# Attention pieces of batches 0 and 1 in another order, in a fused sparse-attention and feed-forward kernel

## The chip, the cores and the metric

The kernel runs on one core of a Trainium2 chip. The core has TensorE for matrix products (PE in the profile, PEld for its weight loads), VectorE (DVE), ScalarE (ACT), GpSimd (POOL) and a queue for transfers (SP), each with its own instruction stream. The metric is the time of one execution on the device in microseconds (us). The kernel before takes 332.97 us (median of three runs, 332.66 to 333.33). A profile of one execution covers a span of 331.5 us; all positions below are counted from the start of that span.

## The reference

Eight batches of eight heads, 576 positions, head dimension 64. Heads 0 to 3 attend to the last 32 positions (local), heads 4 to 7 to earlier positions with the same index modulo 32 (strided). The result goes through a feed-forward layer with a PReLU-like activation.

```python
    scores = scale * np.matmul(q, k.transpose(0, 1, 3, 2))
    pos = np.arange(S)
    rel = pos[:, None] - pos[None, :]
    mask_local = (rel >= 0) & (rel < stride)          # heads 0..3
    mask_strided = (rel >= 0) & (pos[None, :] % stride == pos[:, None] % stride)
    ...
    attn = attn / (np.sum(attn, axis=-1, keepdims=True) + 1e-09)
    return np.matmul(attn, v).astype(np.float32)
...
    h = x @ w_in            # x: (4608, 512), w_in: (512, 2048)
    g = np.maximum(h, 0.0) + alpha * np.minimum(h, 0.0)
    return (g @ w_out).astype(np.float32)
```

## The kernel before, in words

**Units and pairs.** A batch has two units, strided and local, of four heads each. A unit has two pairs of heads; pair g belongs to batch g // 4, and `P.hp` = g % 4 says which (0 and 1 local, 2 and 3 strided). The output of a pair fills one of the four 128-row slabs of `xT`, the input of the feed-forward layer, for the 576 columns of its batch.

**Pieces.** The attention work is cut into closures, the pieces:

- `T(u, "q")`, `T(u, "k")` (`transpose_piece`, L235): eight TensorE transposes of a unit's q or k into a PSUM tile `tp`, then copies to SBUF (`qT`, `kT`). In batches 0 and 1 (`NEARLY = 2`) the copy is in two halves, one for each pair, one on DVE and one on ACT. With k come the last 64 positions (`tails`, PSUM tile `tt`, L258 and L263).
- `Sc(g, i)` (`score_piece`, L295): half of a pair's scores; in batches 0 and 1 the mask is added by two more matmuls (L311). ACT computes the exponential into one of six `et` tiles (L316, L319).
- `Pv(g, i)` (`pv_piece`, L345): probabilities times V, with a column of ones that gives the sum; then DVE's reciprocal `rc` (L352) and division into `x16` (L354). A strided pair has three such pieces, a local pair two.
- `X(g)` (`x_piece`, L362): transposes of `x16` into a PSUM tile `xp`, and a copy to `xT`: on ACT for strided pairs (L366), on DVE for local ones (L370).
- `over_v` (L189): a DVE copy of 32 rows inside the local V tile, which the local PVs read.

The PSUM tiles `tp`, `tt`, `pv` and `xp` share one pool of three buffers (tag `ps`), so each new one needs an old one to be read to its end.

**Order.** `keep` holds every engine's instructions in the order in which the program writes them. The order of pieces for batches 0 and 1 is written out by `alone(u0, u1, ahead)`, called with the strided unit as u0, the local one as u1 and `ahead` true: transposes and scores of the strided unit, transposes of the local unit, scores of its first pair, all six strided PVs, scores of the second local pair, both strided X, the four local PVs (`over_v` ahead of the first), both local X.

**Around it.** Batch 0's pieces run alone on TensorE; after each, `warm` puts matmuls that only keep TensorE busy (`wps`, L608; one of 512 columns from the third piece on). Before the fifth piece DVE casts batch 0's strided V (`cast_v`). Then comes the feed-forward layer in nine chunks of 512 tokens. Its first product is `lin1_piece` (16 pieces of four matmuls into `hps`, L544; ACT's negative part L554, DVE's combination L557). The second is `lin2_piece` (16 pieces of four matmuls into `ops`, L586, with ACT's `osb` copy at each fourth, L591). Batch 1's pieces run between the `lin2` pieces of chunk 0: none after the first, two after each of the next nine, one after each of the last six, and what is left at the end. Later batches are interleaved with later chunks by another loop, which the change doesn't touch.

Of the kernel before, what the change touches and what calls it, by code (L numbers as in the profile page):

```python
# [31 lines left out]
def kernel(  # L32
# [10 lines left out]
    nc = tc.nc  # L43
    keep = tc.keep_in_program_order

    B, H, S, D = q.shape
# [36 lines left out]
    xT = cpool.tile([128, 4, RING], F16)  # L83
# [89 lines left out]
    def cast_copy(eng, o, i):  # L173
        if eng == "act":
            keep(nc.scalar.copy(o, i))  # L175
        elif eng == "dve":
            keep(nc.vector.tensor_copy(o, i))  # L177
        else:
            keep(nc.gpsimd.tensor_copy(o, i))  # L179
# [9 lines left out]
    def over_v(b, eng):  # L189

        v16 = vls[b % 2]
        cast_copy(eng, v16[0:32, 1:24, :], v16[96:128, 0:23, :])
# [7 lines left out]
    NEARLY = 2  # L200

    def make_pair(g):
        P = Pair()
        P.g, P.b, P.hp = g, g // 4, g % 4
        P.strided = P.hp >= 2
        P.pr = P.hp % 2
        P.n, P.w = (8, 72) if P.strided else (6, 96)
        u = g // 2
        P.dx = P.b >= DX and P.strided
        P.xd = P.b >= DX and P.hp < 3  # L210
        if P.dx:
            P.qT, P.kT = (z[u % 2].rearrange("r e c -> r (e c)") for z in (qTs, kTs))
        else:
            P.qT, P.kT = qTs[u % 2][:, g % 2], kTs[u % 2][:, g % 2]
        P.sgroups = ([0, 1, 2, 3], [4, 5, 6, 7]) if P.strided else ([0, 1, 2], [3, 4, 5])
        P.pgroups = ([0, 1, 2], [3, 4, 5], [6, 7]) if P.strided else P.sgroups
        P.et = {}
        P.x16 = None
        return P

    def transpose_piece(u, nm):

        b, strided = u // 2, u % 2 == 1
        early = b < NEARLY
        src = cast16[(b, strided, nm)]
        dst = qTs[u % 2][:, :, 0:576] if nm == "q" else kTs[u % 2][:, :, 32:608]  # L230
        tp = pspool.tile([128, 8, 64, 2], F16, tag="ps", name="tp")
        for j in range(8):
            blk = (src[:, j % 2, 128 * (j // 2) : 128 * (j // 2) + 128] if strided
                   else src[:, j].rearrange("p f d -> p (f d)"))
            keep(nc.tensor.transpose(tp[:, j].rearrange("r p e -> r (p e)"), blk, ident))  # L235
        if strided:
            main = tp.rearrange("r j p e -> r e j p")
            o = dst.rearrange("r e (j p) -> r e j p", j=8)[:, :, :, 0:64]
        else:
            main = tp.rearrange("r t p e -> r e p t")  # L240
            o = dst[:, :, 0:512].rearrange("r e (p t) -> r e p t", t=8)
        if early:
            for e in range(2):
                eng = "dve" if (nm == "q") == (e == 0) else "act"
                if nm == "k" and e == 1:
                    tails(b, u, strided)
                cast_copy(eng, o[:, e : e + 1], main[:, e : e + 1])
            return
        cast_copy("dve" if nm == "q" else "act", o, main)
        if nm == "k":  # L250
            tails(b, u, strided)
# [79 lines left out]
    def pv_piece(P, a):  # L331
        if P.x16 is None:
            if P.xd and P.strided:
                P.x16 = x16s
            else:
                P.x16 = xpool.tile([128, 1024], F16, tag="x16", name="x16")
        v16 = cast16[(P.b, P.strided, "v")]
        grp = P.pgroups[a]
        r = 72 if P.strided else 128
        pv = pspool.tile([128, 512], F32, tag="ps", name="pv")  # L340
        nb = 2 * len(grp)
        for x in range(nb):
            t, hh = grp[x // 2], x % 2
            et, c = P.et[(t, hh)]
            keep(nc.tensor.matmul(  # L345
                pv[:, 65 * x : 65 * x + 65], et[0:r, c : c + 128],
                v16[0:r, 2 * P.pr + hh, t, :] if P.strided else v16[:, 6 * (2 * P.pr + hh) + t, :],
                start=(x == 0), stop=(x == nb - 1), skip_group_check=True))
        w = P.w
        rc = rpool.tile([128, 8], F32, tag="rc", name="rc")  # L350
        pvv = pv[0:w, 0 : 65 * nb].rearrange("r (c e) -> r c e", e=65)
        keep(nc.vector.reciprocal(rc[0:w, 0:nb], pvv[:, :, 64]))  # L352
        c0 = 128 * grp[0]
        keep(nc.vector.tensor_tensor(  # L354
            P.x16[0:w, c0 : c0 + 64 * nb].rearrange("r (c e) -> r c e", e=64),
            pvv[:, :, 0:64],
            rc[0:w, 0:nb].unsqueeze(2).to_broadcast([w, nb, 64]), op=ALU.mult))

    def x_piece(P):
        xp = pspool.tile([128, 1024], F16, tag="ps", name="xp")  # L360
        for t in range(P.n):
            keep(nc.tensor.transpose(  # L362
                xp[:, P.w * t : P.w * t + P.w], P.x16[0 : P.w, 128 * t : 128 * t + 128], ident[0 : P.w, 0 : P.w]))
        base = (P.b % 4) * S
        if P.strided:
            keep(nc.scalar.copy(  # L366
                xT[:, P.hp, base : base + S].rearrange("r (p t) -> r p t", t=8),
                xp[:, 0:576].rearrange("r (t p) -> r p t", t=8)))
        else:
            keep(nc.vector.tensor_copy(xT[:, P.hp, base : base + S], xp[:, 0:576]))  # L370

    def x_dma(P):
        base = (P.b % 4) * S
# [14 lines left out]
    pairs = [make_pair(g) for g in range(npair)]  # L388
    pieces = []

    def feed(fn, g):
        pieces.append((g, fn))

    def T(u, nm):
        return lambda: transpose_piece(u, nm)

    def Sc(g, i):
        return lambda: score_piece(pairs[g], i)

    def Pv(g, i):  # L400
        return lambda: pv_piece(pairs[g], i)

    def X(g):
        return lambda: x_piece(pairs[g])

    def alone(u0, u1, ahead):

        A, L = (2 * u0, 2 * u0 + 1), (2 * u1, 2 * u1 + 1)
        feed(T(u0, "q"), -1)
        feed(T(u0, "k"), -1)  # L410
        for g in A:
            for i in range(2):
                feed(Sc(g, i), -1)
        if ahead:
            feed(T(u1, "q"), -1)
            feed(T(u1, "k"), -1)
            for i in range(2):
                feed(Sc(L[0], i), -1)
        for g in A:
            for i in range(3):  # L420
                feed(Pv(g, i), -1)
        if not ahead:
            feed(T(u1, "q"), -1)
            feed(X(A[0]), -1)
            feed(T(u1, "k"), -1)
            feed(X(A[1]), -1)
            for i in range(2):
                feed(Sc(L[0], i), -1)
        for i in range(2):
            feed(Sc(L[1], i), -1)  # L430
        if ahead:
            for g in A:
                feed(X(g), -1)
        for g in L:
            for i in range(2):
                if g == L[0] and i == 0:
                    feed(lambda: (over_v(u0 // 2, "dve"), pv_piece(pairs[L[0]], 0)), -1)
                else:
                    feed(Pv(g, i), -1)
        for g in L:  # L440
            feed(X(g), -1)

    alone(1, 0, True)
    end0 = len(pieces)
    alone(3, 2, True)
    end1 = len(pieces)


# [307 lines left out]
```

The softmax here doesn't subtract the row's maximum and nothing guards it: scores larger than these inputs give would overflow.

## Time and profile before

| engine | busy us | share of the span |
|---|---|---|
| PE | 319.1 | 96% |
| PEld | 161.6 | 49% |
| DVE | 183.0 | 55% |
| ACT | 171.8 | 52% |
| POOL | 141.2 | 43% |

Batch 0's pieces up to the last strided score take PE to 13.8 us. Its remaining pieces run from there to 27.2 us, where the first full `lin1` chunk sets in. That chunk takes PE to 40.9 us; batch 1's pieces lie between 42.5 and 66.6 us. A matmul's record shows its start well, while its end is modelled; a chain piece such as "PE tp L235 x8" gives the time by which eight matmuls move the chain on. "ACT kT L175 waited for" means that the engine named first stood until that instruction ended. Line 175 is the ACT branch and line 177 the DVE branch of the copy helper, so these lines are told apart by the tile's name.

### The profile page before, as it was taken

What the parts mean: (1) busy time and instruction counts of PE and PEld (TensorE: products, weight loads), DVE (VectorE), ACT (ScalarE), POOL (GpSimd) and SP (SyncE); (2) the same over time, 40 slices, a digit from 0 to 9 for tenths busy, and PEclk for the clock granted to TensorE, in tenths of its full rate; (3) what the DMA queues carried; (4) which work ended last, traced back from release to release, by engine and by line L of the source; (5) the groups of instructions that cost most, each with busy time, mean ns of one, the idle gap of its engine ahead of it and who ended that gap; (6) DMA issues with size and microseconds to landing.
All of it is one profiled execution on the core that took longest, in us unless ns stands there. A gap on an engine that the chain in (4) does not pass through costs nothing.

```text
span 331.5 us, 6272 instructions
## 1 busy us (share of the span) xinstructions
PE 319.1 (96%) x2493; PEld 161.6 (49%) x2493; DVE 183.0 (55%) x358; ACT 171.8 (52%) x297; POOL 141.2 (43%) x152
## 2 busy tenths in 40 slices
PE   7899999999998999999999999999999999999995
PEld 2554455554553445444458654445444444444444
DVE  5477836477544873387428832783368238605800
ACT  2644753458456645575457544764477237415611
POOL 7932495117986366736583628332611400000000
PEclk9999999999999999999999999999999999999999
DMA  7999999699599459774978397517730130011011
GB/s 221 194 205 206 248 207 154 109 211 210 105 159 179 163 69 162 122 203 55 172 114 216 37 153 125 106 17 106 139 57 18 51 96 21 1 74 52 2 63 63
DMA packets 77596, 40.32 MB, mean 122 GB/s; under 512 B 58480, under 2 KB 69248, under 8 KB 77568
## 3 DMA queue, kind: packets, MB, share of 16 engines
q0 software_dynamic: 41728, 17.38, 49.6%
q1 hardware_dynamic: 35840, 22.55, 29.9%
q8 instruction: 19, 0.31, 0.4%
q14 instruction: 9, 0.07, 0.1%
HBM read 38.01 MB, written 9.44 MB: 143 GB/s over the span
## 4 chain that ended last, share of the span: by engine, by line
PE 89%; ACT 4%; DVE 3%; DMA 2%; issue 1%; SPq 0%; ACTq 0%
PE hps L544 37%; PE ops L586 37%; PE sp L295 4%; PE pv L345 4%; PE tp L235 2%; DMA kl<-in_k_dram 2%; DVE x L354 1%; PE wps L608 1%; PE ops L577 1%; ACT xT L366 1%; ACT osb L591 1%; PE sph L311 1%; PE sp L311 1%; ACT kT L175 1%; DVE qT L177 1%
## 5 line engine op out<-in xcount | busy, mean ns | idle before, releaser
L544 PE MATMUL hps<-xT,win 128*128 128x512 f16 (+1 forms) x640 | 134.1, 358 | 3.4 <-ACT xT L366 2.8
L586 PE MATMUL ops<-wout,gT 128*128 128x512 f16 x560 | 137.0, 379 | 0.0
L557 DVE SCALAR_TENSOR_TENSOR gT<-neg,oma,hps 128x512 f16<-128x512 f32 x144 | 105.9, 744 | 51.3 <-ACT neg L554 43.6
L554 ACT ACTIVATE neg<-hps 128x512 f32<-128x512 f32 x144 | 86.0, 597 | 46.3 <-PE hps L544 45.2
L329 POOL TENSOR_TENSOR et<-et,consts 128x576 f16<-128x576 f16 (+1 forms) x48 | 61.1, 1275 | 94.3 <-ACT et L319 94.2
L544 PEld LDWEIGHTS <-win 128*128 128x128 f16 x640 | 59.6, 98 | 60.8 <-issue 7.3
L586 PEld LDWEIGHTS <-gT 128*128 128x128 f16 x560 | 48.3, 98 | 45.9
L319 ACT ACTIVATE et<-sp 72x576 f16<-72x576 f32 (+1 forms) x56 | 36.2, 646 | 30.9 <-PE sp L295 17.0
L591 ACT COPY osb<-ops 128x512 f32<-128x512 f32 x35 | 20.5, 586 | 49.9 <-PE ops L586 46.0
L352 DVE RECIPROCAL rc<-pv 72x6 f32<-72x6 f32 (+2 forms) x80 | 14.9, 186 | 55.0 <-PE pv L345 54.9
L354 DVE TENSOR_TENSOR x<-pv,rc 96x384 f16<-96x384 f32 (+2 forms) x62 | 33.0, 532 | 2.1
L345 PEld LDWEIGHTS <-et 72*128 72x128 f16 (+1 forms) x448 | 23.6, 98 | 16.8 <-DVE x L354 1.1
L295 PEld LDWEIGHTS <-kT 64*128 64x128 f16 x448 | 10.8, 95 | 26.2 <-issue 21.2
L295 PE MATMUL sp<-qT,kT 64*128 64x72 f16 (+1 forms) x392 | 17.0, 201 | 1.9 <-ACT kT L175 1.9
L608 PE MATMUL wps<-wrm 128*128 128x512 f16 x44 | 16.2, 442 | 1.2 <-DVE wrm L620 1.2
L177 DVE COPY qT<-tp 128x1024 f16<-128x1024 f16 (+1 forms) x10 | 10.1, 1010 | 11.7 <-PE tp L235 11.7
L167 POOL DMA_DIRECT2D vl<-in_v_dram x8 | 11.2, 1396 | 11.8 <-PE xp L362 10.5
L345 PE MATMUL pv<-vs,et 72*128 72x65 f16 x256 | 15.2, 194 | 0.1
L179 POOL COPY vs<-stv 72x1024 f16<-72x1024 f16 x14 | 14.4, 1034 | 0.0
L175 ACT COPY kT<-tp 128x1024 f16<-128x1024 f16 (+1 forms) x10 | 8.4, 843 | 7.4 <-PE tp L235 7.4
L383 ACT COPY xT<-xs 128x576 f16<-128x576 f16 x6 | 7.8, 1302 | 7.6 <-DMA xs<-x16s 7.6
L345 PE MATMUL pv<-vl,et 128*128 128x65 f16 x192 | 11.1, 194 | 0.0
(73 smaller groups left out, 162.9 us busy)
## 6 DMA issues: line engine op xcount, KB each, us to landing
out_dram<-osb SPq DMA_DIRECT2D x35, 256.0 KB, 2.3
ql<-in_q_dram SPq DMA_DIRECT2D x6, 512.0 KB, 5.9
kl<-in_k_dram SPq DMA_DIRECT2D x6, 512.0 KB, 6.3
stv<-in_v_dram POOLq DMA_DIRECT2D x8, 288.0 KB, 7.1
vl<-in_v_dram POOLq DMA_DIRECT2D x6, 384.0 KB, 10.6
win<-in_moe_w_in_dram POOLq DMA_DIRECT2D x4, 512.0 KB, 9.5
wout<-in_moe_w_out_dram POOLq DMA_DIRECT2D x4, 512.0 KB, 17.1
qsd<-in_q_dram POOLq DMA_DIRECT2D x6, 288.0 KB, 6.2
```

What stands on the lines that cost most here:

```text
L295: keep(nc.tensor.matmul(sps[y][:, w * x : w * x + w], P.kT[hf, k0 : k0 + 128], P.qT[hf, q0 : q0 + w], start=(x == 0), stop=(x == len(grp) ...
L319: keep(nc.scalar.activation(ev.rearrange("r (y c) -> r y c", y=2), sp[0:r, :, 0:n], AF.Exp, scale=SCALE))
L329: keep(nc.gpsimd.tensor_tensor(ev, ev, m, op=ALU.mult))
L345: keep(nc.tensor.matmul(pv[:, 65 * x : 65 * x + 65], et[0:r, c : c + 128], v16[0:r, 2 * P.pr + hh, t, :] if P.strided else v16[:, 6 * (2 * ...
L352: keep(nc.vector.reciprocal(rc[0:w, 0:nb], pvv[:, :, 64]))
L354: keep(nc.vector.tensor_tensor(P.x16[0:w, c0 : c0 + 64 * nb].rearrange("r (c e) -> r c e", e=64), pvv[:, :, 0:64], rc[0:w, 0:nb].unsqueeze ...
L544: keep(nc.tensor.matmul(hps[:, dst : dst + w], win16[:, kk, 128 * m : 128 * m + 128], xT[:, kk, src : src + w], start=(kk == 0 and x == 0) ...
L554: keep(nc.scalar.activation(neg, hps, AF.Relu, scale=-1.0))
L557: keep(nc.vector.scalar_tensor_tensor(gTs[n][:, m, :], neg, oma[:, m : m + 1], hps, op0=ALU.mult, op1=ALU.add))
L586: keep(nc.tensor.matmul(ops, gTs[n][:, kf, 128 * mt : 128 * mt + 128], wout16[:, kf, :], start=(kf == 0), stop=(kf == 15)))
L591: keep(nc.scalar.copy(osb, ops))
L608: keep(nc.tensor.matmul(wps, wrm[:, 0:128], wrm, start=True, stop=True))
```

## The change

`alone` loses its third parameter and writes one list. The strided PVs no longer come in one block: those of the first strided pair lie around the local transposes, those of the second between the local scores. `over_v` comes ahead of the second strided pair's first PV instead of the first local PV. Local PVs start ahead of the strided X pieces and alternate with them. In addition the `xT` copy of local pair 0 goes to ACT instead of DVE in batches 0 and 1. Which pieces exist, and how many, is as before.

Order of batch 0 and 1 from the seventh piece on (A0, A1: strided pairs; L0, L1: local pairs):

- before: Tq, Tk, Sc L0 (2), Pv A0 (3), Pv A1 (3), Sc L1 (2), X A0, X A1, over_v + Pv L0 (2), Pv L1 (2), X L0, X L1
- after: Pv A0, Tq, Pv A0, Tk, Pv A0, Sc L0 (2), over_v + Pv A1, Sc L1, Pv A1, Sc L1, Pv A1, Pv L0, X A0, Pv L0, X A1, Pv L1 (2), X L0, X L1

```diff
@@ x_piece
-            keep(nc.vector.tensor_copy(xT[:, P.hp, base : base + S], xp[:, 0:576]))
+            cast_copy("act" if P.b < NEARLY and P.hp == 0 else "dve",
+                      xT[:, P.hp, base : base + S], xp[:, 0:576])
@@ alone
-    def alone(u0, u1, ahead):
+    def alone(u0, u1):
 
         A, L = (2 * u0, 2 * u0 + 1), (2 * u1, 2 * u1 + 1)
-        feed(T(u0, "q"), -1)
-        feed(T(u0, "k"), -1)
-        for g in A:
-            for i in range(2):
-                feed(Sc(g, i), -1)
-        if ahead:
-            feed(T(u1, "q"), -1)
-            feed(T(u1, "k"), -1)
-            for i in range(2):
-                feed(Sc(L[0], i), -1)
-        for g in A:
-            for i in range(3):
-                feed(Pv(g, i), -1)
...
-        for i in range(2):
-            feed(Sc(L[1], i), -1)
-        if ahead:
-            for g in A:
-                feed(X(g), -1)
-        for g in L:
-            for i in range(2):
-                if g == L[0] and i == 0:
-                    feed(lambda: (over_v(u0 // 2, "dve"), pv_piece(pairs[L[0]], 0)), -1)
-                else:
-                    feed(Pv(g, i), -1)
-        for g in L:
-            feed(X(g), -1)
-
-    alone(1, 0, True)
+        fns = [T(u0, "q"), T(u0, "k")] + [Sc(g, i) for g in A for i in range(2)]
+        fns += [Pv(A[0], 0), T(u1, "q"), Pv(A[0], 1), T(u1, "k"), Pv(A[0], 2), Sc(L[0], 0), Sc(L[0], 1)]
+        fns += [lambda: (over_v(u0 // 2, "dve"), pv_piece(pairs[A[1]], 0)), Sc(L[1], 0), Pv(A[1], 1)]
+        fns += [Sc(L[1], 1), Pv(A[1], 2), Pv(L[0], 0), X(A[0]), Pv(L[0], 1), X(A[1])]
+        fns += [Pv(L[1], 0), Pv(L[1], 1), X(L[0]), X(L[1])]
+        for fn in fns:
+            feed(fn, -1)
+
+    alone(1, 0)
     end0 = len(pieces)
-    alone(3, 2, True)
+    alone(3, 2)
```

More of the change, by code (lines that the diff above doesn't have):

```diff
@@ L404, in X @@
         return lambda: x_piece(pairs[g])
-    def alone(u0, u1, ahead):
+    def alone(u0, u1):
         A, L = (2 * u0, 2 * u0 + 1), (2 * u1, 2 * u1 + 1)
-        feed(T(u0, "q"), -1)
-        feed(T(u0, "k"), -1)
-        for g in A:
-            for i in range(2):
-                feed(Sc(g, i), -1)
-        if ahead:
-            feed(T(u1, "q"), -1)
-            feed(T(u1, "k"), -1)
-            for i in range(2):
-                feed(Sc(L[0], i), -1)
-        for g in A:
-            for i in range(3):
-                feed(Pv(g, i), -1)
[L422 to L426, printed above, removed]
-            for i in range(2):
-                feed(Sc(L[0], i), -1)
-        for i in range(2):
-            feed(Sc(L[1], i), -1)
-        if ahead:
-            for g in A:
-                feed(X(g), -1)
-        for g in L:
-            for i in range(2):
-                if g == L[0] and i == 0:
-                    feed(lambda: (over_v(u0 // 2, "dve"), pv_piece(pairs[L[0]], 0)), -1)
-                else:
-                    feed(Pv(g, i), -1)
-        for g in L:
-            feed(X(g), -1)
-    alone(1, 0, True)
+        fns = [T(u0, "q"), T(u0, "k")] + [Sc(g, i) for g in A for i in range(2)]
[6 more added lines that the diff above has]
+    alone(1, 0)
     end0 = len(pieces)
-    alone(3, 2, True)
+    alone(3, 2)
     end1 = len(pieces)
```

## The prediction, written before the result was known

> **What bounds the kernel now.** I read the table of engines first, then the chain that ended last with its pieces in order of time, then the timeline and the waits of the stretch that the change rewrites.
>
> ```profile
> PE 319.1 (96%) x2493; PEld 161.6 (49%) x2493; DVE 183.0 (55%) x358; ACT 171.8 (52%) x297; POOL 141.2 (43%) x152
> ...
> PE 89%; ACT 4%; DVE 3%; DMA 2%; issue 1%; SPq 0%; ACTq 0%
> ```
>
> TensorE (PE) carries 89% of the chain. Only idle time of PE can be won, and after batch 0 there is little of it. So I look where the chain leaves PE, between 13.8 and 27.2 us, batch 0's own stage (start, length, piece):
>
> ```profile
> 13.81 0.46 PE tp L235 x8
> 14.29 0.70 DVE qT L177
> 15.02 0.59 ACT qT L175
> 15.61 0.50 ACT kT L175
> ...
> 18.26 0.55 DVE x L354
> 18.95 0.56 DVE x L354
> ...
> 25.70 0.56 DVE x L354
> 26.31 0.32 PE xp L362 x3
> 26.65 0.47 DVE xT L370
> 27.16 13.76 PE hps L544 x63
> ```
>
> There are three detours. The local scores follow the local transposes at once and wait for four copies. The divisions of six strided PVs come in one lump, and DVE serves one per 0.69 us (18.26 to 18.95). The last division, transposes and copy are a tail. The waits of 13.8 to 27.2 us agree (total, times, longest):
>
> ```profile
> PEld L362 <- DVE x L354: 1.3, 3, 0.5
> ...
> PEld L345 <- DVE x L354: 1.1, 4, 0.4
> PE sp L295 <- ACT kT L175: 0.9, 1, 0.9
> ```
>
> PE's work in this stretch, from the chain: 19 warm matmuls at 0.22 (4.1), two transpose pieces and a tail (0.92 + 0.12), four score pieces at 0.58 (2.3), six strided PVs (four at 0.20, two at 0.13: 1.06), four local PVs at 0.20 (0.8), X pieces 2 x 0.26 + 2 x 0.31 (1.14): 10.5 us. The stretch takes 27.16 - 13.81 = 13.35, so **2.9 us is idle**. Batch 1 runs the same pieces beside lin2 groups of 0.86, which hide nearly all; its row of PE waits is 0.8 for kT and 0.5 for the last division.
>
> **What the Trainium skill says.** "PSUM — Partial Sum Buffer", section "PSUM bank collisions raise a hardware error", says that ScalarE and VectorE must not read one bank at once, so the two halves of a transposed tile are copied one after the other. The trace agrees: the ACT half of qT starts at 15.02, when DVE's ends at 14.98. The same page, "Engine vs sequencer instructions", calls the queues of ScalarE and VectorE strictly first in, first out and matmuls in program order. The trace agrees: in no view did I see one overtake another. Hence a PV's division placed between two copies delays the later copy. Nothing else here rests on a page.
>
> **The change, part by part.** Instruction counts don't change: 26 pieces per batch before and after, the same copies, one of the two local xT copies moved from DVE to ACT. Pieces 1 to 6 stay, so batch 0 is equal up to 13.81. I then placed each piece by hand: PE in order, each piece followed by a warm matmul of 0.22; DVE in order with reciprocal plus division at 0.69 (0.54 for four blocks); ACT copies at 0.48 to 0.59. The transposes, PVs and X pieces share three PSUM buffers and take the one that was released longest ago (the PV at 18.87 waits for the first division, which ends at 18.81).
>
> - First strided PV at 13.81. It needs DVE's V casts: they start at 12.81, when the strided V lands, and end by 13.77. No wait, but no slack either; before, it ran at 17.65. Division to 14.80.
> - qT transposes 14.23 to 14.69; DVE half from 14.73, ACT half 15.45 to 16.04. Second PV 14.91; division to 16.13.
> - kT transposes 15.33 to 15.79. Their tail tile takes the buffer of the q transposes, held until 16.04: **a new PE wait of about 0.3 us**. Behind it queue the third PV and the local scores. The tail copies end at 16.76.
> - Third PV 16.42. Local scores at 16.81 instead of 16.15, but 0.64 us of strided PV work and three warm matmuls are already done. The wait for kT shrinks from 1.06 (15.09 to 16.15) to almost nothing.
> - over_v (0.54 on DVE, the row of 22.01) at about 17.75. The local V was issued at 6.63 and takes 9.5 to land: 16.13, so 1.6 us of slack. It delays only a reciprocal. Cost zero.
> - PVs of the second strided head pair at 18.42, 19.64 and 20.86, a score piece between each two. DVE has 1.2 us for each 0.69: the 1.1 us of buffer waits goes.
> - Then local PV 21.21, X 21.63, PV 22.11, X 22.53, PV 23.01, PV 23.43. ACT takes the strided X copies, so DVE holds only divisions. The last division starts at 24.15, since that of the PV before ends at 24.00, and ends at 24.70.
> - Tail: last three transposes 24.75 to 25.07, DVE's xT to 25.56, lin1 goes on at 25.60. The xT copy moved to ACT (0.64, as for the strided ones) runs 24.2 to 24.8 beside it. In the old trace that copy on DVE ended (26.64) when the last transposes did (26.62), so moving it saves nothing by itself.
>
> Batch 0: 27.16 - 25.60 = **1.56 us**. Bounds: if the last division never waits behind the one before (PV ends at 23.63), lin1 starts at 25.28, 1.9 us; if the tail-tile wait is twice as long and every later piece shifts by it and by one more division of 0.69, about 0.6.
>
> Batch 1, one or two pieces per lin2 group: before, PE stood about 0.47 at 51.1 to 51.58 for kT. Now PVs and two lin2 groups lie between; left is some 0.1 for the tail tile. The first kT wait (0.37 at 45.1) and the tail after the last PV (64.89 to 66.59) have the same pieces as before. Gain **0.35** (0 to 0.5).
>
> Do the inputs follow an earlier PE? The next strided q and k were issued at 18.14 and 20.69 and land after 19.6 and 18.6 us: 37.7 and 39.3. Their tails land by 39.7. PE will want them at 40.9, 41.4 and 41.9. GpSimd's V casts of batch 1 end at 44.5; the PV that is now early comes at 47.7. Its local k cast ends at 47.8; wanted at 49.4. The local V lands at 49.7; over_v comes at 54. All fit, with 1.2 us the least. From 66 us on PE is the chain in long stretches and the later loads are issued from the pieces themselves, so the shift should last to the end.
>
> Sum: 1.56 + 0.35 = 1.9 of 332.97 gives **331.1 us**.
>
> **Rivals.**
> - *Half of it* (chance 0.2). The queue of DVE and the three PSUM buffers give new waits: copies wedged between divisions, X tiles waiting for ACT. For: transposes and PVs now alternate in one pool, and I had margins of 0.2 us at two X pieces. Against: DVE's work in the stretch falls to 9.2 of 11.8 us. Keeping the 1.3 us of waits before transposes and adding 0.7, of 2.9: gain 0.9, or 332.1.
> - *No change* (0.07). PE gets to batch 1 early and waits there for the loads, which keep their own pace: the DMA rows were busy until 60 us. For: the tails of batch 1 land 2.2 us before their use. Against: all slacks above are positive. Time 332.9.
> - *Slower* (0.08). The first PV now stands at the head of PE's queue with no slack on the strided V. Should V land 2.5 us later (its next loads took 12.1 and 12.9 us, not 7.5), local transposes, scores and all else wait behind it; so lost 2.5 - 1.9 + 0.2 of knock-on: 333.8. Against: the load's issue and its company on the queues don't change.
> - *Forecast* (0.65): 331.1.
>
> **How the numbers follow.** Half a gain still is over 0.2% (0.67 us) mostly: faster 0.83, same 0.09, slower 0.08. The range starts at the sum of the upper bounds (1.9 + 0.5, 330.5, with 0.1 of scatter, 330.4) and ends at 332.5, past the half case, leaving out the no-change and slower cases.
>
> **What would show it.** lin1 (hps) starts at 25.6, not 27.16; the PE wait of scores for kT at 16 us is gone and a short PE wait of tt for ACT's qT stands in its place; buffer waits of strided PVs vanish; the PE wait before 51.58 falls to 0.1; later gaps keep their lengths. The prediction is wrong if the first PV waits for the V cast, if over_v waits for its load, or if batch 1's first transposes wait for DMA.

## The result and the profile after

The changed kernel takes **331.32 us** (median of 6 runs, 330.88 to 331.43), the kernel before beside it 332.94 (332.66 to 333.33): a ratio of 0.9949 with a 95% interval of 0.9936 to 0.9962. It is faster by 1.6 us. The forecast was 331.1.

First the table of engines and the chain by engine, from the page of the changed kernel:

```profile
PE 318.7 (97%) x2493; PEld 162.2 (49%) x2493; DVE 183.9 (56%) x356; ACT 173.4 (53%) x299; POOL 141.1 (43%) x152
...
PE 91%; ACT 3%; DVE 2%; DMA 2%; issue 1%; SPq 0%; ACTq 0%
```

The work is the same, and the chain has gone two points further onto PE. Where that came from is seen in the chain's pieces in order of time (start, length, piece), over the same stretch as before. The changed kernel's file is 25 lines shorter, so `hps` is L519 here and was L544, and the `xT` copy of a local pair now goes through the copy helper (L175 on ACT, L177 on DVE):

```profile
13.76 0.20 PE pv L345 x6
...
14.21 0.55 DVE x L354
14.77 0.61 DVE qT L177
15.38 0.02 issue
15.40 0.59 ACT qT L175
15.99 0.04 issue
16.04 0.27 PE tt L263 x2
...
23.51 0.55 DVE x L354
24.07 0.11 DVE rc L352
24.18 0.02 issue
24.20 0.57 DVE x L354
24.77 0.05 issue
24.82 0.32 PE xp L362 x3
25.13 0.02 issue
25.15 0.47 DVE xT L177
25.62 0.04 issue
25.66 13.76 PE hps L519 x63
```

Two detours are left of three. The first is the new one: division, DVE half of q, ACT half of q, and the tail tile that waits for their buffer (16.04). Between 16.31 and 23.26 the chain stays on PE, where before it went through DVE's divisions. The second is the old end, two divisions, three transposes and one copy. The feed-forward layer goes on at 25.66 (before 27.16; forecast 25.60). Batch 1 ends at 64.94 (before 66.59). The waits of the stretch, in the same columns as before (total, times, longest):

```profile
PEld L362 <- DVE x L354: 0.7, 2, 0.5
...
PE tt L263 <- ACT qT L175: 0.4, 1, 0.4
PE xp L362 <- DVE x L354: 0.3, 1, 0.3
```

The weight loads' waits of PVs for divisions (1.1 before) and the scores' wait for kT (0.9) are in no row any more; the tail tile's wait is new.

The two profiled spans, 331.5 and 329.3, differ by 2.2 us, 0.6 more than the medians. That surplus arises after batch 1 and is taken up below: it belongs to one transfer and not to the change.

To compare profiles whose first loads land a few tenths apart, I cut every execution at three points: the start of the mask matmuls in the last strided score piece, ahead of the new order (13.17 before, 13.13 after), the time when chunk 0's product goes on (27.16, 25.66) and the same for chunk 1 (66.59, 64.94).

| run | batch 0 stage | batch 1 stage | from there to the end | median time |
|---|---|---|---|---|
| before | 13.99 | 39.43 | 264.9 | 332.94 |
| after | 12.53 | 39.28 | 264.4 | 331.32 |
| after, again | 12.55 | 39.27 | 263.9 | 331.47 |
| batch 0 only | 12.56 | 39.44 | 264.6 | 331.36 |
| V rows late | 13.88 | 39.84 | 265.0 | 333.23 |
| X first | 13.07 | 39.27 | 264.2 | 331.70 |
| end alone | 13.41 | 39.44 | 264.7 | 332.15 |
| copy on DVE | 12.53 | 39.27 | 264.2 | 331.41 |
| q whole on ACT | 12.21 | 38.97 | 264.3 | 330.88 |
| q first | 12.64 | 39.29 | 264.9 | 331.83 |

The stages repeat to 0.03 us where code and order are equal. The change brings 1.46 in batch 0 and 0.15 in batch 1: 1.61 of the 1.62 that the medians show.

### The profile page after: what moved, and what is told of

The parts are those of the page before. It is cut to its first block, busy times and chain, and to the rows that moved or that the text cites. A ratio compares the mean times of both kernels' runs of the same rounds, so it can differ in the third digit from the quotient of the medians.

```text
span 329.3 us, 6276 instructions
## 1 busy us (share of the span) xinstructions
PE 318.7 (97%) x2493; PEld 162.2 (49%) x2493; DVE 183.9 (56%) x356; ACT 173.4 (53%) x299; POOL 141.1 (43%) x152
## 4 chain that ended last, share of the span: by engine, by line
PE 91%; ACT 3%; DVE 2%; DMA 2%; issue 1%; SPq 0%; ACTq 0%
PE hps L519 37%; PE ops L561 37%; PE sp L295 4%; PE pv L345 4%; PE tp L235 2%; PE wps L583 2%; DMA ql<-in_q_dram 2%; PE ops L552 1%; ACT xT L366 1%; ACT osb L566 1%; PE sph L311 1%; PE sp L311 1%; DVE x L354 1%; DVE qT L177 1%; PE sph L295 1%
## 5 line engine op out<-in xcount | busy, mean ns | idle before, releaser
L519 PE MATMUL hps<-xT,win 128*128 128x512 f16 (+1 forms) x640 | 133.9, 358 | 3.2 <-ACT xT L366 2.6
L519 PEld LDWEIGHTS <-win 128*128 128x128 f16 x640 | 59.6, 98 | 60.3 <-issue 6.7
L345 PEld LDWEIGHTS <-et 72*128 72x128 f16 (+1 forms) x448 | 24.4, 98 | 16.4
L177 DVE COPY qT<-tp 128x1024 f16<-128x1024 f16 (+1 forms) x10 | 10.1, 1007 | 7.1 <-PE tp L235 7.1
L175 ACT COPY kT<-tp 128x1024 f16<-128x1024 f16 (+1 forms) x10 | 8.4, 842 | 7.4 <-PE tp L235 7.4
```

Of the source, the lines that this page charges most:

```text
L345: keep(nc.tensor.matmul(pv[:, 65 * x : 65 * x + 65], et[0:r, c : c + 128], v16[0:r, 2 * P.pr + hh, t, :] if P.strided else v16[:, 6 * (2 * ...
L519: keep(nc.tensor.matmul(hps[:, dst : dst + w], win16[:, kk, 128 * m : 128 * m + 128], xT[:, kk, src : src + w], start=(kk == 0 and x == 0) ...
```

## The experiments

The kernel before beside these runs took 333.00 us in the first group of four, 333.01 in the second and 333.15 in the last two.

### Batch 0 only

```diff
-            cast_copy("act" if P.b < NEARLY and P.hp == 0 else "dve",
+            cast_copy("act" if P.b == 0 and P.hp == 0 else "dve",
...
         fns += [Pv(L[1], 0), Pv(L[1], 1), X(L[0]), X(L[1])]
+        if u0 == 3:
+            fns = [T(u0, "q"), T(u0, "k")] + [Sc(g, i) for g in A for i in range(2)]
+            fns += [T(u1, "q"), T(u1, "k"), Sc(L[0], 0), Sc(L[0], 1)] + [Pv(g, i) for g in A for i in range(3)]
...
```

> New order (and the copy on ACT) in batch 0 alone, batch 1 in the old order. My theory: batch 0 brings 1.5 us and batch 1 only 0.15, so 331.5 us; chunk 0's first product starts at 25.7 as with the whole change, batch 1 ends at 65.1 instead of 64.9. Rival, batch 1's order carries a real share (the 0.35 that I forecast, or more): 331.7 to 332.1, batch 1 ends at 65.3 or later.

Measured: 331.36 us, ratio 0.9952 (0.9938 to 0.9965). Batch 0's stage is that of the whole change (12.56), batch 1's that of before (39.44). So batch 1's new order is worth 0.16 us by the stage; the timed runs (331.36 and 331.32) can't tell so little. My 0.35 was too much. The rival for batch 1 falls.

### V rows copied late

```diff
-        fns += [lambda: (over_v(u0 // 2, "dve"), pv_piece(pairs[A[1]], 0)), Sc(L[1], 0), Pv(A[1], 1)]
+        fns += [Pv(A[1], 0), Sc(L[1], 0), Pv(A[1], 1)]
-        fns += [Sc(L[1], 1), Pv(A[1], 2), Pv(L[0], 0), X(A[0]), Pv(L[0], 1), X(A[1])]
+        fns += [Sc(L[1], 1), Pv(A[1], 2), lambda: (over_v(u0 // 2, "dve"), pv_piece(pairs[L[0]], 0)), X(A[0]), Pv(L[0], 1), X(A[1])]
```

> The whole change, but the V rows are copied at the first local PV again, as before. My theory: the copy then queues on DVE behind the division that ends at 21.7, so the first local PV waits on PE from 21.2 to 22.2; plus 0.95 us in batch 0 and plus 0.4 in batch 1: 332.6 us. Rival, the place of a 0.54 us copy is indifferent because PE has other work: 331.3.

Measured: 333.23 us, ratio 1.0007 (0.9999 to 1.0015): **the whole gain is gone**. PE's waits between 13.3 and 28 us begin with

```profile
PE pv L345 <- DVE vl L177: 1.1, 1, 1.1
```

and the first local PV, started at 21.24, goes on at 22.48. Batch 0's stage grows by 1.35 (forecast 0.95), batch 1's by 0.56 (0.4). Of the 0.4 more in batch 0, some 0.2 is another thing: in this execution the strided V landed half a microsecond later and DVE began its casts at 13.27 instead of 12.75; the first PV started at 13.75, 0.67 after the last scores, where the others take 0.47 to 0.51. This is the risk I had named for the first PV, on a small scale. The other 0.2 isn't traced. The direction and the mechanism are as expected: the V rows' place is a condition of the rest of the change.

### Strided X first

```diff
-        fns += [Sc(L[1], 1), Pv(A[1], 2), Pv(L[0], 0), X(A[0]), Pv(L[0], 1), X(A[1])]
+        fns += [Sc(L[1], 1), Pv(A[1], 2), X(A[0]), X(A[1]), Pv(L[0], 0), Pv(L[0], 1)]
```

> The whole change, but both strided X pieces ahead of the local PVs, as before. My theory: the four local PVs then come every 0.42 us while DVE needs 0.69 each, and the last division ends later: plus 0.45 us in batch 0, nothing in batch 1 (one piece per group of the second product): 331.75 us, chunk 0 starts at 26.1. Rival, the order at the end is indifferent, because the gain comes from the strided PVs between the transposes: 331.3, chunk 0 at 25.7.

Measured: 331.70 us, ratio 0.9961 (0.9949 to 0.9974). Chunk 0 goes on at 26.34; batch 0's stage is 0.54 longer (forecast 0.45), batch 1's the same. DVE's timeline of this run (start, length, engine and instruction, and in brackets the idle time before it) shows where the half microsecond goes:

```profile
21.43 0.42 DVE L354 TENSOR_TENSOR x<-pv,rc 72x256 f16<-72x256 f32 x1
22.58 0.19 DVE L352 RECIPROCAL rc<-pv 96x6 f32<-96x6 f32 x1 [0.73 <-PE pv L345]
22.81 0.55 DVE L354 TENSOR_TENSOR x<-pv,rc 96x384 f16<-96x384 f32 x1
23.28 0.18 DVE L352 RECIPROCAL rc<-pv 96x6 f32<-96x6 f32 x1
```

DVE stands idle for 0.73 us while PE does the strided X pieces, and then has four local divisions back to back. With a PV ahead of each X piece that hole is filled: in the changed kernel DVE goes on at 21.59, right behind this division, and its next hole is 0.20 (before 23.29). The half microsecond is read from the stages; the medians (331.70 against 331.32 and 331.47) leave it between 0.2 and 0.4.

### The later part alone

```diff
-        fns += [Pv(A[0], 0), T(u1, "q"), Pv(A[0], 1), T(u1, "k"), Pv(A[0], 2), Sc(L[0], 0), Sc(L[0], 1)]
-        fns += [lambda: (over_v(u0 // 2, "dve"), pv_piece(pairs[A[1]], 0)), Sc(L[1], 0), Pv(A[1], 1)]
-        fns += [Sc(L[1], 1), Pv(A[1], 2), Pv(L[0], 0), X(A[0]), Pv(L[0], 1), X(A[1])]
+        fns += [T(u1, "q"), T(u1, "k"), Sc(L[0], 0), Sc(L[0], 1), Pv(A[0], 0), Pv(A[0], 1), Pv(A[0], 2)]
+        fns += [lambda: (over_v(u0 // 2, "dve"), pv_piece(pairs[A[1]], 0)), Pv(A[1], 1), Pv(A[1], 2)]
+        fns += [Sc(L[1], 0), Sc(L[1], 1), Pv(L[0], 0), X(A[0]), Pv(L[0], 1), X(A[1])]
```

> Only the later part of the change: transposes, local scores of the first pair and all strided PVs in the old order; V rows copied ahead of the fourth strided PV, local PVs ahead of strided X, copy on ACT. My theory: the wait for kT at 16 us and the buffer waits of the PVs come back, but DVE no longer stands idle before the local PVs, so about half of batch 0's gain stays: 332.15 us, chunk 0 starts at 26.4; batch 1 has its 0.45 us wait for kT again. Rival, the gain is all from the strided PVs between transposes and scores: 333.0, chunk 0 at 27.1.

Measured: 332.15 us, ratio 0.9978 (0.9970 to 0.9986). Batch 0 keeps 0.58 of its 1.46, and both the PVs' waits for divisions and the wait for kT are back:

```profile
PEld L345 <- DVE x L354: 0.9, 3, 0.4
PE sp L295 <- ACT kT L175: 0.9, 1, 0.9
```

Batch 1's stage is that of before. So the place of the strided PVs brings 0.88 in batch 0 on top of the later part, and all of batch 1's gain. The parts don't add, though: without its V rows in place the change brings 0.11 in batch 0 (13.99 against 13.88), or some 0.3 if the late landing in that execution is taken off.

### The local copy on DVE again

```diff
-            cast_copy("act" if P.b < NEARLY and P.hp == 0 else "dve",
-                      xT[:, P.hp, base : base + S], xp[:, 0:576])
+            cast_copy("dve", xT[:, P.hp, base : base + S], xp[:, 0:576])
```

> The whole change, but the xT copy of local pair 0 on DVE again. My theory: it runs while PE does the last transposes of pair 1, so the time is the same: 331.3 us, chunk 0's first product at 25.7. Rival, the copy on ACT is worth its 0.46 us in each of the two batches: 331.8 to 332.2.

Measured: 331.41 us, ratio 0.9958 (0.9946 to 0.9970); both stages equal to the whole change within 0.01. The copy's move to ACT is worth nothing.

### Local q copied whole by ACT

```diff
+        if early and not strided and nm == "q":
+            cast_copy("act", o, main)
+            return
         if early:
             for e in range(2):
```

> The whole change, and the local q transposes of batches 0 and 1 are copied by ACT in one instruction instead of half by DVE and then half by ACT. My theory: the wait of the tail tile for the buffer of the q transposes is on the path (0.45 us in batch 0 with the restart of the matmuls, 0.25 in batch 1); one copy of about 1.0 us that doesn't queue behind a division ends half a microsecond earlier, and the wait is gone: 330.6 us, chunk 0 at 25.15. Rival, another wait takes its place at once (scores for kT, a division): 331.3, chunk 0 at 25.6.

Measured: 330.88 us (330.68 to 330.90), ratio 0.9932 (0.9920 to 0.9945), against 331.47 for the changed kernel beside it. Batch 0's stage is 0.32 shorter (forecast 0.5) and batch 1's 0.31 (forecast 0.25). PE's matmuls of the k unit in batch 1, first of the changed kernel and then of this run (start, modelled length):

```profile
49.27 0.61 PE L235 MATMUL tp<-consts,kl 128*128 128x128 f16 x8
50.02 0.27 PE L263 MATMUL tt<-consts,tl 128*128 128x128 f16 x2
```

```profile
49.25 0.61 PE L235 MATMUL tp<-consts,kl 128*128 128x128 f16 x8
49.70 0.28 PE L266 MATMUL tt<-consts,tl 128*128 128x128 f16 x2
```

Where nothing holds it up, the tail tile starts 0.45 us after the k transposes; in the changed kernel it starts 0.75 after, so that wait cost 0.30, and all of it is won. In batch 0 ACT's copy runs from 14.95 to 15.96 and the tail tile starts at 16.02, 0.65 after the k transposes, so 0.2 of the wait stays. "The wait is gone" holds for batch 1 alone.

### Local q first

```diff
-        fns += [Pv(A[0], 0), T(u1, "q"), Pv(A[0], 1), T(u1, "k"), Pv(A[0], 2), Sc(L[0], 0), Sc(L[0], 1)]
+        fns += [T(u1, "q"), Pv(A[0], 0), Pv(A[0], 1), T(u1, "k"), Pv(A[0], 2), Sc(L[0], 0), Sc(L[0], 1)]
```

> The whole change, but the local q transposes ahead of the first strided PV, and two strided PVs between q and k. My theory: in batch 0 the k transposes instead of the tail tile now wait for the q buffer, no change, and batch 1 gets back 0.25 us: 331.1 us. Rival, the first PV at the head of the queue costs time because it waits for the V cast: then this is faster by more than 0.3 us already in batch 0, and chunk 0 starts at 25.3 or earlier.

Measured: 331.83 us, ratio 0.9961 (0.9947 to 0.9975): not faster than the change, and my forecast is refuted for batch 1. There the stage is 39.29, nothing gained: PE's waits show the k transposes waiting for ACT's half of q (0.2) in place of the tail tile. Batch 0's stage is 0.11 longer, so the rival, a cost of the V cast at the head of PE's queue, falls too for executions in which V lands on time. The remaining 0.25 of the median isn't in these stages; this run's profile has a long wait of the kind that follows.

### The changed kernel again, and the wait before chunk 2

> The changed kernel again, as the base for the runs beside it: 331.3 us. In its first profile ACT's wait for a transposed strided block at 99 us was 0.46 us shorter than in the profile before. My theory: that is scatter of the transfer, not the change; so that wait differs between profiles of equal kernels. Rival, the change shortens it: the same 2.4 us here.

Measured: 331.47 us, ratio 0.9955 (0.9944 to 0.9967). ACT's wait for the transposed block before chunk 2 was 2.9 us in the profile before and 2.4 after. The same row of the waits from 95 to 106 us, for the equal kernel:

```profile
ACT xT L384 <- DMA xs<-x16s: 1.9, 1, 1.9
```

So that wait differs by half a microsecond between equal kernels. Over the ten profiles above it runs from 1.9 to 3.0, and the last stage of the table follows it: less the wait, the last column but one is 262.0 in each of them, within 0.1. It accounts for 0.5 of the 0.6 by which the two spans differ more, and the timed medians need none of it, since the two stages add up to 1.61. The three kernels that lack most of the gain (before, V rows late, end alone) have waits of 2.7 to 3.0, but each of these profiled executions took 0.4 to 0.5 us more than its kernel's median, so that is no sign of an effect of the order.

To see whether the wait is on the path, the exponential behind it was put ahead of it:

```diff
-                if copyp and 4 * DX <= g - 2 < npair and pairs[g - 2].xd and pairs[g - 2].strided:
-                    x_copy(pairs[g - 2])
+                for r, here in ((g - 3, kind == "S" and g < npair), (g - 2, copyp and g == npair)):
+                    if here and 4 * DX <= r < npair and pairs[r].xd and pairs[r].strided:
+                        x_copy(pairs[r])
```

> The changed kernel, and from batch 2 on ACT's copy of a transposed strided block stands behind the next pair's first exponential instead of ahead of it. Nothing of batches 0 and 1 is touched. My theory: the spread of equal kernels comes from ACT's wait for that block before chunk 2 (1.9 to 3.0 us in ten profiles), because the exponential (0.64 us), the output copy and an xT copy queue behind it and TensorE waits for the last; with the exponential ahead of the wait, chunk 2 goes on about 0.55 us earlier: 330.85 us. Rival, TensorE would wait as long for something else there: 331.4.

Measured: 331.09 us, ratio 0.9944 (0.9930 to 0.9957). Against the two medians of the changed kernel (331.32, 331.47) the time fell by 0.2 to 0.4 instead of 0.55, and the intervals overlap, so the timed runs don't decide it. The time from chunk 1's start to chunk 2's doesn't decide it either: it is 37.21 here, and 37.50 and 37.06 in the two profiles of the changed kernel, because the block lands at another time in each. What decides it is the time from the start of the block's copy to chunk 2's first product on the new input. First the changed kernel, then this run:

```profile
99.52 1.30 ACT L384 COPY xT<-xs 128x576 f16<-128x576 f16 x1 [2.39 <-DMA xs<-x16s]
102.44 2.10 PE L519 MATMUL hps<-xT,win 128*128 128x512 f16 x9 [0.95 <-ACT xT L366]
```

```profile
99.77 1.31 ACT L384 COPY xT<-xs 128x576 f16<-128x576 f16 x1 [0.44 <-DMA xs<-x16s]
102.15 2.10 PE L520 MATMUL hps<-xT,win 128*128 128x512 f16 x9 [0.64 <-ACT xT L366]
```

That is 2.92 us and 2.38. In all ten profiles above it is 2.92 or 2.93, while the copy starts anywhere from 98.79 to 102.02. So chunk 2 follows this block, and the exponential taken out of the queue behind it is worth 0.54 us for an equal landing, as forecast; the rival falls. From chunk 2 to the end both executions take 226.9, so nothing behind it eats the gain. The scatter of the landing stays, since the output copy and the xT copy still stand behind the block: the five runs of this kernel spread as widely (330.91 to 331.36) as the first six of the change. The two profiled executions of the changed kernel took 331.28 and 330.52 us; of these 0.76 us, 0.27 arise ahead of chunk 0 and 0.44 between chunk 1 and chunk 2. For the other runs the share of this wait in the spread isn't shown.

### Both

> The run before this one together with the local q transposes copied whole by ACT in batches 0 and 1. My theory: the gains lie in stretches that don't overlap (before 65 us and at 100 us), so they add: 0.6 + 0.55 less than the changed kernel, 330.25 us. Rival: an earlier batch 1 only lengthens the wait at 100 us, so that the first gain is lost there: 330.85.

Measured: **330.15 us** (330.05 to 330.31), ratio 0.9913 (0.9900 to 0.9927), 1.3 less than the changed kernel in the run again. The stages are 12.2 and 38.96, as with q whole on ACT, and from chunk 1's start to chunk 2's is 36.90. Alone the two brought 0.59 and 0.38, so together they bring at least their sum, and the rival falls. What goes beyond the sum may be the transfer: in this profile the block had landed before ACT came to it (98.47, copy at 98.58), so ACT didn't wait for it at all. This is the fastest version here.

## Why the prediction was right

- **The bound.** PE idle time in batch 0's stage was what there was to win; the work of PE didn't change and the time did. Right.
- **The wait for kT and the buffer waits.** Both went, as the waits show, and with the order of the strided PVs undone both came back (end alone). Right.
- **The tail tile's new wait.** It came at the place and by the cause forecast (the tile starts at 16.04, when I had its buffer come free): the Trainium skill, "PSUM — Partial Sum Buffer", section "PSUM bank collisions raise a hardware error", doesn't allow ScalarE and VectorE on one bank at the same time, and ACT's half starts at 15.40 when DVE's ends at 15.38. Its size was off. I took 0.3 us from 15.79, which is the chain's end of the k transposes; before the change the chain has the q transposes end at 14.27, while the next matmul starts at 14.09. From starts to starts, 15.07 + 0.45 = 15.52 against 16.04, it is 0.5. Since the place of the tile itself was right, what follows is off by 0.1 at most.
- **The first PV.** It didn't wait, but "no slack" was a misreading. DVE casts the strided V in two instructions, one for each pair, and the first PV reads only the first. In the changed kernel that one ends at 13.17 and the PV starts at 13.60, ahead of the second's end at 13.70. So there were some 0.4 us of slack, and V landing half a microsecond late cost only 0.2 (V rows late).
- **over_v at no cost.** Right at its new place (17.77, in DVE's hole ahead of the fourth strided PV's division), and the runs show more than I said: at the old place the copy takes back the whole gain.
- **The end.** Last division 24.20 to 24.77 (forecast 24.15 to 24.70), chunk 0 at 25.66 (25.60); the copy on ACT is worth nothing, as derived.
- **Batch 0: 1.56 forecast, 1.46 measured** by the stage, 1.50 by absolute times. Right. One sum on the way has a slip: the strided PV work done ahead of the local scores is 0.20 + 0.20 + 0.13 = 0.53, not 0.64.
- **Batch 1: 0.35 forecast, 0.15 measured.** The term that was mis-sized is the difference of two waits. TensorE's timeline, first before and then after:

```profile
50.09 1.03 PE L586 MATMUL ops<-wout,gT 128*128 128x512 f16 x4
51.58 0.30 PE L295 MATMUL sp<-qT,kT 64*128 64x96 f16 x6 [0.47 <-ACT kT L175]
```

```profile
50.99 0.29 PE L345 MATMUL pv<-vs,et 72*128 72x65 f16 x4
51.21 0.30 PE L295 MATMUL sp<-qT,kT 64*128 64x96 f16 x6
```

By starts the old wait for kT was 0.63 (the group that starts at 50.09 takes 0.86, the scores start at 51.58), not 0.47. The new wait of the tail tile is 0.30, not 0.1. The scores without a wait start 0.1 after their turn (51.21 after a PV of 0.12 that starts at 50.99), which the old wait had covered. And one group of the second product starts 0.07 late (53.40 after a PV of 0.18 at 53.15). 0.63 - 0.30 - 0.10 - 0.07 = 0.16, as the run with batch 0 only has it.
- **The shift lasts to the end.** The last stage depends on the one transfer, not on the order. Right. No PE wait of batch 1 names a load, so the rival "no change" has nothing for it. The least slack among those listed for the loads is 1.6 us (k cast, 47.8 to 49.4), not 1.2.
- **The other rivals.** "Half of it" named new waits, and two came: the tail tile's, and one of the second strided X piece for a division (0.36 in the chain where the first X takes 0.26). Together they are far from taking half. "Slower" showed its mechanism once, with 0.2 us (V rows late).

## What to carry to other kernels

Place the pieces by hand, engine by engine, with measured durations and the release order of shared buffers: here that gave the time of the next stage within 0.1 us. Measure a wait on TensorE from matmul start to matmul start, since ends are modelled: the tail tile's wait is 0.36 us as a gap between records and 0.52 by starts. When two engines take turns on one PSUM bank, splitting its copy between them need not free it earlier: here the local q took 0.68 us on DVE and then 0.58 on ACT, behind a division, and 1.01 whole on the idle ACT. Where a consumer needs only the first half, a split can still pay: the first local scores (16.80) start while DVE still copies the other half of kT (16.50 to 17.19); no run here tests k copied whole. And put a small copy that later work needs where its engine has a hole: the same 0.54 us cost nothing in one place and the whole gain in another.

## What the runs showed that I had not expected

In batch 1 the copy of the V rows took longer at its new place. Before, and then in the changed kernel's run again, DVE's timeline has:

```profile
57.87 0.54 DVE L177 COPY vl<-vl 32x1495 f16<-32x1495 f16 x1
```

```profile
51.70 2.31 DVE L177 COPY vl<-vl 32x1495 f16<-32x1495 f16 x1
```

In the eight profiles in which it starts between 51.4 and 52.7 us it took 0.54 to 2.31 us (1.49 in the first profile of the change); it took 0.54 in the four in which it starts at 55.4 or later. I had put it at 54 us, where its PV stands; DVE came to it two microseconds earlier, and there GpSimd casts q and k. In the changed kernel's run again:

```profile
51.56 1.06 POOL L179 CAST ql<-ql 128x1024 f16<-128x1024 f32 x1
52.55 1.05 POOL L179 CAST kl<-kl 128x1024 f16<-128x1024 f32 x1
```

The copy ends at 54.01, 0.41 us after the second cast. So it is in all seven profiles in which it took longer than 0.54: its end lies 0.40 to 0.42 us behind the end of one of these casts. In the one profile of the eight in which it started between the two casts (51.99, in the run with the block's copy later, where no cast runs from 51.73 to 52.41) it took 0.54. And in the three profiles in which it got in between casts that follow each other closely (q whole on ACT, q first, both), the second cast takes 1.38 or 1.39 us instead of 1.04 to 1.06. So copy and casts exclude each other here. The Trainium skill, "SBUF — State Buffer", section "Who interferes with whom", says that VectorE copies in the two-port modes and GpSimd lock each other out of a shared port. The measured times agree with that; that this copy ran in such a mode is not shown. It cost nothing, because DVE had a hole: batch 1's stage is 39.27 with 2.31 us and 39.28 with 1.49.
